# Attention with v as scaled float16 pairs, the logits kept in other tiles, and x's rows split at other steps

## The chip, the cores and the metric

The kernel runs on one core of a Trainium2 chip. The metric is the device time of one execution in microseconds (us); the median of the runs stands for the kernel. The trace is that of one further execution, taken by the hardware profiler. Engines: PE is TensorE (PEld its weight loads), DVE is VectorE, ACT is ScalarE, POOL is GpSimd; SPq is the queue in which SyncE issues the transfers (DMAs).

## What is computed

Attention with a decay, an MLP with h·cos(h), and a dense mixture of eight experts whose gates are made doubly stochastic:

```python
scores = scale * q @ k.T + (cum[:, None] - cum[None, :])   # causal; 4 batches, 8 heads, 576 rows, 64 columns
x = softmax(scores) @ v                                    # -> 2304 x 512
h = x @ w_in                                               # 512 -> 2048
x = (h * cos(h)) @ w_out                                   # 2048 -> 512
P = sinkhorn(exp(x @ w_gate))                              # 2304 x 8, eight rounds
out = sum(P[:, e:e+1] * (relu(x @ w1[e]) @ w2[e]) for e in range(8))
```

The answer is in float32, so the large matmuls split each operand into a high and a low half and add three products (hi·hi, hi·lo, lo·hi).

## The kernel before, in words

There are three stages. **Attention** handles 16 pairs of heads, seven steps to a pair, 112 steps in all. Steps 0 to 5 of a pair are the row tiles [0, 1], [2], [3] of head 0 and then of head 1; step 6 is the last 64 rows of both heads. The loop over x (from L818) writes out by hand what each engine does at a step: `on_pe`, `on_act`, `on_dve`, then `go("pool", x)`. Every engine works in its written order, and an instruction that waits holds up all that are behind it on its engine. The table `PREP` (L516) says at which step before or after its own first step (that of pair 0 in the second place) and on which engine each piece of a pair's preparation is emitted.

For pair n, `load_pair(n + 2)` (L341 on, with the copies at L330, L336 and L340) is emitted at the pair's step 2: ten DMAs in the SP queue, four for q, three for k, three for v. Ahead of it in the same step and the same queue stands `dq1` (L553), a DMA that copies what ACT wrote by `qhi1` (L489, the 640 columns of the second head of q, emitted one step earlier). The raw v lies in one of three tiles. `square_v` (L466) squares v on ACT and sums it into a column of `vsum`; it is emitted four steps ahead of its pair. `split_v` (L448) makes three bfloat16 parts of v on POOL in five instructions. `weigh` (L673) multiplies the two float16 halves of the attention weights with those parts, five matmuls to a block of 128 by 128 (L701); the last 64 rows go in float32 (L681). `norm` (L704) divides by the row sums.

```python
"v_sq": (("act", -4), ("act", -3)),
"ld": (("pool", 2), ("pool", 2)),
ACT_ORDER = ("XEH", "EXH", "EXH", "XHE", "XEH", "XEH", "XEH")
```

In these letters X is the preparation, E the exponentials of the next step (L639), H the high half of the weights of this step (L663, L659).

Between the steps, `pieces` prepares the MLP's weights: `read_unit` (L168) reads 64-bit words into float32 with four DVE instructions for each of two halves (L175, L177, L179, L182, with a product on POOL at L174), and after the third of them asks for the next weights by `load_job` (L122, L127), a DMA in the SP queue that waits until DVE has read the staging tile. One unit of weights takes some four pairs. `chunk_scale` and `split_row` (L223) scale and split x, the MLP's input, on POOL, as each of the five chunks of rows becomes complete; a chunk has four row blocks, three POOL instructions each.

**The MLP** runs 80 items (4 blocks of units, 5 chunks, 3 to 5 units) in order: `layer1` (12 matmuls, L263), `between` (ACT and DVE, L282 to L290), `layer2` two items later (12 matmuls, L943). The first two `layer1` are emitted in the last attention steps. `survey` (L893) reads the experts' weights for their largest values into the two tiles `seen`. In the last block `logits` (L991) multiplies x by the gate's weights and copies the result into a tile `lg`, which lies in `tmw1` or `tmw2`, tiles of the weight reader; `logits2` (L1005) turns it.

**The experts** start with POOL alone: `prepare_alone` (L1208 to L1271) splits the first four parts of the experts' weights, and `combine_first` (L1291 to L1295) makes seven sums of x blocks, all in POOL's written order. Their tiles lie in the memory that the MLP's tiles leave. The tile of the second part, `wa01`, lies on bytes 148256 to 155424 of a partition; on the same bytes lay the end of `xl1` (134240 to 150624, the operand of `logits` for chunks 1 and 3), `tmw1` (150624 to 154720) and the start of `tmw2` (from 154720).

Of the kernel before, what the change touches and what calls it, by code (L numbers as in the profile page):

```python
# [23 lines left out]
def kernel(  # L24
# [75 lines left out]
    wsum = [big.tile([P, 2], F32, name=f"wsum{i}") for i in range(3)]  # L100
    vsum = big.tile([P, B * HP], F32, name="vsum")
    xsum = big.tile([P, NCH], F32, name="xsum")
    bk_w, sc_w = [big.tile([P, NUM, 2], F32, name=nm) for nm in ("bkw", "scw")]
    bk_x, sc_x = [big.tile([P, NCH], F32, name=nm) for nm in ("bkx", "scx")]
    both, lift = [big.tile([P, NUM], F32, name=nm) for nm in ("both", "lift")]
# [187 lines left out]
    with tc.manual_schedule():  # L293

        with ExitStack() as actx:
# [20 lines left out]
            K1 = [ap1.tile([P, S], F32R, name=f"k1_{i}") for i in range(4)]  # L316
            K2 = [ap1.tile([P, S], F32R, name=f"k2_{i}") for i in range(4)]
            E4 = ap1.tile([P, SP], F32, name="e4")
            vraw = [ap1.tile([P, NQ, 2, D + 1], F32, name=f"vraw{i}") for i in range(3)]
            qraw = [ap1.tile([P, NQ, 2 * D], F32, name=f"qr{i}") for i in range(2)]  # L320
            kraw = [ap1.tile([P, NQ, 2 * D], F32, name=f"kr{i}") for i in range(2)]
# [110 lines left out]
            nc.gpsimd.memset(qraw[1][LAST:P, NQ - 1, 0:D], 0.0)  # L432
            for t in (kraw[1], xpt):
                nc.gpsimd.memset(t[LAST:P, NQ - 1, :], 0.0)
            for i in range(3):
                nc.gpsimd.memset(vraw[i][:, :, :, D : D + 1], 1.0)
                nc.gpsimd.memset(vraw[i][LAST:P, NQ - 1, :, :], 0.0)
# [7 lines left out]

            vs_of, tr_of = {}, {}

            def split_v(n):  # L448
                vr = raw[n][2]
                v1 = ap2.tile([P, NF, 2, D + 1], BF16, tag="v1", name="v1")  # L450
                v23 = ap2.tile([P, 2, NF, 2, D], BF16, tag="v23", name="v23")
                rest = ap1.tile([P, NF, 2, D], F32, tag="tmp", name="vrest")
                vs_of[n] = (v1, v23[:, 0], v23[:, 1])
                nc.gpsimd.tensor_scalar(v1, vr[:, 0:NF], 1.0, 0.0, ALU.mult, ALU.add)
                nc.gpsimd.tensor_tensor(rest, vr[:, 0:NF, :, 0:D], v1[:, :, :, 0:D], ALU.subtract)
                yield
                nc.gpsimd.tensor_scalar(v23[:, 0], rest, 1.0, 0.0, ALU.mult, ALU.add)
                nc.gpsimd.tensor_tensor(rest, rest, v23[:, 0], ALU.subtract)
                yield
                nc.gpsimd.tensor_scalar(v23[:, 1], rest, 1.0, 0.0, ALU.mult, ALU.add)  # L460
                done.add(("v", n))
                yield

# [29 lines left out]
            def lo_in(n, which, h):  # L493
# [32 lines left out]
                "dk0": (("pool", -5), ("dve", -4)),  # L526
                "ql0": (("dve", -7), ("dve", -4)),
                "kl0": (("pool", -5), ("dve", -4)),
                "sp0": (("pool", -3), ("pool", -3)),
                "sp1": (("pool", -2), ("pool", -2)),  # L530
                "ql1": (("dve", -5), ("dve", -2)),
                "sp2": (("pool", -2), ("pool", -2)),
                "v_sq": (("act", -4), ("act", -3)),
                "ld": (("pool", 2), ("pool", 2)),
                "x_act": (("act", 11), ("act", 11)),
                "dq0": (("dma", -7), ("pool", -4)),
# [136 lines left out]
            def weigh(x):  # L673
                n, y = divmod(x, PS)
                h, ts = KIND[y]
                A = A_of.pop(x)
                if h is None:
                    for hh in range(2):
                        for kt in range(NQ):
                            c = kt * P + hh * LAST  # L680
                            nc.tensor.matmul(  # L681
                                pv_of[n, 1][0:LAST, NF + hh, :], A[:, c : c + LAST], raw[n][2][:, kt, hh, :],
                                start=kt == 0, stop=kt == NQ - 1,
                            )
                    return
                if ts[0] == 0:
                    bank = ps_o.tile([P, 512], F32, tag="o", name="pv")
                    spare_bank[:] = [lambda: bank[:, (NF + 2) * (D + 1) :]]
                    pv_of[n, h] = bank[:, 0 : (NF + 2) * (D + 1)].rearrange("p (t d) -> p t d", d=D + 1)
                need(("v", n))  # L690
                v1, v2, v3 = vs_of[n]
                c = 0
                for t in ts:
                    todo = []
                    for kt in range(t + 1):
                        hi, lo = A[:, 0, c : c + P], A[:, 1, c : c + P]
                        w1, w2, w3 = v1[:, kt, h, :], v2[:, kt, h, :], v3[:, kt, h, :]
                        todo += [(hi, w1), (hi, w2), (hi, w3), (lo, w2), (lo, w1)]
                        c += P
                    for y, (a, w) in enumerate(todo):  # L700
                        nc.tensor.matmul(  # L701
                            pv_of[n, h][:, t, 0 : w.shape[1]], a, w, start=y == 0, stop=y == len(todo) - 1
                        )

            def norm(n, h):
                if h == 0:
                    xp_of[n] = xpt
                xp, pv = xp_of[n], pv_of.pop((n, h))
                rc = RC[h]
                parts = [(P, 0, NF, xp[:, 0:NF, h * D : (h + 1) * D], ESC)]  # L710
                if h == 1:
                    parts.append((LAST, NF, NF + 2, xp[0:LAST, NF, :].rearrange("p (h d) -> p h d", h=2), 1.0))
                for m, t0, t1, _, esc in parts:
                    nc.vector.tensor_scalar(rc[0:m, t0:t1, :], pv[0:m, t0:t1, D : D + 1], 1e-9 * esc, None, ALU.add)
                nc.vector.reciprocal(rc, rc)
                for m, t0, t1, dst, _ in parts:
                    nc.vector.tensor_tensor(
                        dst, pv[0:m, t0:t1, 0:D], rc[0:m, t0:t1, :].to_broadcast([m, t1 - t0, D]), ALU.mult
                    )
# [16 lines left out]
            def put(n, key, fn, *args):  # L736
                eng, step = PREP[key][n == 0]
                ON["pool" if eng == "dma" else eng].setdefault(n * PS + step, []).append((RANK[key], fn, args))
# [14 lines left out]
            for n in range(NPAIR):  # L753
                if n:
                    put(n, "aug", aug, n)
                put(n, "q_pe", turn_in, n, 0)
                put(n, "k_pe", turn_in, n, 1)
                for h in range(2):
                    put(n, f"qhi{h}", hi_in, n, 0, h)
                    put(n, f"khi{h}", hi_in, n, 1, h)  # L760
                    put(n, f"dq{h}", dup_in, n, 0, h)
                    put(n, f"dk{h}", dup_in, n, 1, h)
                    put(n, f"ql{h}", lo_in, n, 0, h)
                    put(n, f"kl{h}", lo_in, n, 1, h)
                if "pool" in (eng_of(n, "kl0"), eng_of(n, "kl1")):
                    put(n, "ktc", keep_k, n)
                put(n, "sp0", start_split, n)
                put(n, "sp1", more_split, n)
                put(n, "sp2", more_split, n)
                put(n, "v_sq", square_v, n)  # L770
                put(n, "ld", load_pair, n + 2)
                put(n, "x_pe", turn_x, n)
                put(n, "x_act", keep_x, n)
            pieces = chain(chain.from_iterable(run_unit(u) for u in range(NWA)), read_unit(NWA), scale_unit(NWA))
            scaling = iter(())
            rows = []
            for j, (_, b1) in enumerate(BATCHES):
                first_step = (HP * b1 + HP - 1) * PS
                for x in range(KD):
                    rows.append((max((HP * b1 + x) * PS + 12, first_step + 1), j, x))  # L780
            rows.sort()

            def on_pe(x):
                for z in PE_ORDER[x % PS]:
# [18 lines left out]
            def on_dve(x):  # L803
                n, y = divmod(x, PS)
                for z in DVE_ORDER[x % PS]:
# [8 lines left out]
                    if z == "O" and 0 <= x < NSTEP:  # L814
                        lo_a(x)

            ahead = {}
            for x in range(-9, NSTEP + PS):  # L818
                for n, when in enumerate((NSTEP - 2, NSTEP + 1)):
                    if x == when:  # L820
                        ahead[n] = layer1(*items[n])
                on_pe(x)
                if x == NSTEP + 2:
                    between(*items[0], ahead[0])
                on_act(x)
                on_dve(x)
                go("pool", x)
                quiet[0] = x % PS in (1, 2, 4, 5) or x >= NSTEP
                for j, (_, b1) in enumerate(BATCHES):
                    if x == (HP * b1 + HP - 1) * PS - 3:  # L830
                        scaling = chain(scaling, chunk_scale(j))
# [3 lines left out]
                    next(scaling, None)  # L835
                if rows and rows[0][0] <= x:
                    split_row(*rows.pop(0)[1:])
                if x == NSTEP - 2:
                    quiet[0] = True
                    for _ in scaling:  # L840
                        pass
                    for u in range(NWA):
                        turn_factors(u, 0, NCH)
                    block_factors(0)
                    down_factors(0, 0, NCH)
            quiet[0] = True
            for _ in pieces:
# [138 lines left out]
        def logits(j, xt, step, bank):  # L986
            n = CH[j][1]
            ps = bank()
            for kk in range(KD):
                for s in range(2):  # L990
                    nc.tensor.matmul(  # L991
                        ps[:, 0:n], wg_of[0][:, kk, :], xt[:, s, kk, :], start=kk + s == 0, stop=kk == KD - 1 and s == 1
                    )
            lg = tmw[j % 2 + 1][:, 0:512]
            nc.scalar.copy(lg[0:16, 0:n], ps[0:16, 0:n])
            if step is not None:
                at(after_l2, step, lambda: logits2(j, lg, bank))
# [77 lines left out]
            at(after_l2, 73 + x // 2, lambda x=x: scale_first(x))  # L1075
        pieces = work()
        for n in range(len(items) + LAG):
            if n < len(items):
                ps = ahead.pop(n) if n in ahead else layer1(*items[n])
            for fn in after_l1.pop(n, []):  # L1080
# [625 lines left out]
```

## Time and profile before

| | |
|---|---|
| median of 3 runs | 2045.49 us (2044.63 to 2045.53) |
| the profiled execution | 2045.4 us, its span in the trace 2043.7 us |
| PE, PEld busy | 95%, 68% of the span |
| DVE, ACT, POOL busy | 72%, 59%, 55% |
| attention | to about 252 us |
| MLP | to about 655 us |
| experts | to the end |

Busy time is counted over the whole span, and the three stages have different limits. A matmul's end is modelled, so a PE that is shown as busy need not be at its peak.

### The profile page before, as it was taken

To read this page: it belongs to the slowest core of one execution; us is meant where nothing else is said; L and a number is where in the kernel's file an instruction comes from. 1 tells how busy PE (TensorE), PEld (TensorE's weight loads), DVE (VectorE), ACT (ScalarE), POOL (GpSimd) and SP (SyncE) were. 2 spreads that over 40 slices of the span, in tenths; PEclk is the share of its full clock that TensorE was granted. 3 is DMA by queue.
4 is the path that set the end of the run, shared out by engine and by line. 5 is a ranking of instruction groups with operands and counts; after the bars stand their busy time and mean duration, and the time that the engine had idled before them with its cause. 6 is when DMAs were issued, how large, how long until landed. Compare 5 with 4: busy or idle time off the path is not lost.

```text
span 2043.7 us, 39956 instructions
## 1 busy us (share of the span) xinstructions
PE 1949.8 (95%) x15098; PEld 1393.0 (68%) x15098; DVE 1473.5 (72%) x3237; ACT 1212.3 (59%) x2449; POOL 1126.0 (55%) x1528
## 2 busy tenths in 40 slices
PE   7999989999997489999999999999999999999998
PEld 6888745454543266777777777777777777777776
DVE  8888767786565247878777777777777777777776
ACT  7888778777643266555555555555555555555543
POOL 7888854423022988546555555465555555655531
PEclk9999999999999689999999999999999999999999
DMA  5435255454300202120220211212202122022022
GB/s 130 109 89 116 53 175 176 155 165 125 114 11 11 85 33 100 41 86 32 76 75 22 86 46 62 86 32 76 76 22 86 33 75 86 22 83 78 12 86 63
DMA packets 133921, 157.59 MB, mean 77 GB/s; under 512 B 63840, under 2 KB 98016, under 8 KB 133728
## 3 DMA queue, kind: packets, MB, share of 16 engines
q1 hardware_dynamic: 133728, 155.03, 25.0%
q8 instruction: 119, 1.95, 0.4%
q14 instruction: 74, 0.61, 0.1%
HBM read 139.71 MB, written 10.37 MB: 73 GB/s over the span
## 4 chain that ended last, share of the span: by engine, by line
PE 77%; DVE 7%; POOL 7%; ACT 6%; issue 2%; DMA 0%; SPq 0%; DVEq 0%; POOLq 0%; ACTq 0%
PE y L1571 18%; PE y L1450 17%; PE bq L1571 14%; PE bq L1450 13%; PE ph L263 5%; PE a L943 5%; PE pv L701 1%; PE pst L651 1%; DVE ph L287 1%; ACT t L285 1%; DVE acc L959 1%; PE pss L594 1%; DVE t L284 1%; PE pss L595 1%; DVE tmw L182 1%
## 5 line engine op out<-in xcount | busy, mean ns | idle before, releaser
L1571 PEld LDWEIGHTS <-h 128*128 128x128 f16 x6048 | 592.7, 98 | 87.1 <-POOL h L1485 10.8
L1450 PEld LDWEIGHTS <-wa 128*128 128x128 f16 x4032 | 395.7, 98 | 294.9 <-issue 43.1
L1450 PE MATMUL y<-xc,wa 128*128 128x384 f16 x2304 | 434.5, 328 | 31.4 <-POOL xc L1291 26.6
L1485 POOL TENSOR_TENSOR h<-rt,h 128x384 f16<-128x384 f32 x192 | 175.7, 915 | 449.2 <-ACT h L1484 441.4
L1571 PE MATMUL y<-wb,h 128*128 128x256 f16 x3456 | 410.5, 273 | 10.0 <-POOL h L1485 10.0
L1466 ACT ACTIVATE ct<-y 128x384 f32<-128x384 f32 x192 | 94.4, 491 | 451.5 <-PE y L1450 451.5
L1450 PE MATMUL bq<-xc,wa 128*128 128x384 f16 x1728 | 331.3, 328 | 1.1 <-POOL xc L1292 1.0
L1571 PE MATMUL bq<-wb,h 128*128 128x256 f16 x2592 | 308.2, 273 | 0.2 <-DVE h L1476 0.2
L1552 DVE SCALAR_TENSOR_TENSOR acc<-y,gate,acc 128x256 f32<-128x256 f32 x504 | 212.6, 477 | 48.7 <-PE y L1571 48.6
L943 PE MATMUL a<-H,w 128*128 128x512 f16 (+1 forms) x960 | 203.0, 359 | 9.3 <-ACT H L288 4.3
L263 PE MATMUL ph<-xt,w 128*128 128x512 f16 (+1 forms) x960 | 199.8, 358 | 0.0
L1552 DVE SCALAR_TENSOR_TENSOR acc<-bq,gate,acc 128x256 f32<-128x256 f32 x378 | 159.7, 478 | 39.2 <-PE bq L1571 39.1
L943 PEld LDWEIGHTS <-w 128*128 128x128 f16 x960 | 93.4, 98 | 105.5 <-issue 14.8
L1476 DVE TENSOR_TENSOR h<-bq,h 128x384 f16<-128x384 f32 x288 | 158.1, 551 | 3.2 <-ACT h L1473 0.6
L1470 DVE SCALAR_TENSOR_TENSOR bq<-bq,ct 128x384 f32<-128x384 f32 x192 | 107.7, 561 | 68.2 <-PE bq L1450 67.4
L1470 DVE SCALAR_TENSOR_TENSOR bq<-y,ct 128x384 f32<-128x384 f32 x96 | 54.3, 566 | 140.6 <-PE y L1450 135.3
L263 PEld LDWEIGHTS <-w 128*128 128x128 f16 x960 | 93.6, 99 | 89.5
L1473 ACT CAST h<-bq 128x384 f16<-128x384 f32 x288 | 134.6, 483 | 14.2 <-DVE bq L1527 14.0
L1479 POOL TENSOR_TENSOR h<-st,h 128x384 f16<-128x384 f32 x96 | 88.0, 917 | 84.1 <-ACT h L1473 80.2
L1483 ACT ACTIVATE rt<-bq 128x384 f32<-128x384 f32 x192 | 93.7, 488 | 27.8 <-DVE bq L1470 25.1
L1231 POOL TENSOR_TENSOR tm<-sg 128x256 f32<-128x256 f32 x128 | 92.3, 732 | 15.0 <-POOL h L1479 12.3
L1484 ACT ACTIVATE h<-bq 128x384 f16<-128x384 f32 x192 | 94.3, 491 | 0.0
(260 smaller groups left out, 3214.7 us busy)
## 6 DMA issues: line engine op xcount, KB each, us to landing
xc<-xd SPq DMA_DIRECT2D x105, 384.0 KB
seen<-in_moe_w_dram SPq DMA_DIRECT2D x64, 512.0 KB
sg<-in_moe_w_dram SPq DMA_DIRECT2D x64, 512.0 KB
stg<-in_moe_w_in_dram SPq DMA_DIRECT2D x16, 512.0 KB
stg<-in_moe_w_out_dram SPq DMA_DIRECT2D x16, 512.0 KB
xd<-xc SPq DMA_DIRECT2D x14, 384.0 KB
q<-q SPq DMA_DIRECT2D x30, 160.0 KB
out_dram<-acc SPq DMA_DIRECT2D x18, 256.0 KB
```

The source lines that it names most:

```text
L263: nc.tensor.matmul(ps[:, 0:n], w[:, ws, kk * P : (kk + 1) * P], XT[j][:, xs, kk, :], start=first, stop=kk == KD - 1 and (ws, xs) == PASSES ...
L943: nc.tensor.matmul(a_of[b, j][x][:, 0:n], w[:, s1, DM + x * P : DM + (x + 1) * P], H[:, s2, 0:n], start=i == 0 and n_ == 0, stop=end and n ...
L1450: nc.tensor.matmul(ps[:, 0:HN], w[:, ws, a, k, :], X[b][:, xs, k, :], start=fresh and n == 0, stop=n == 5, skip_group_check=not fresh,)
L1466: nc.scalar.activation(c, cut(ps), AF.Copy, scale=RAISE)
L1470: nc.vector.scalar_tensor_tensor(cut(c), cut(ps), RAISE, other, ALU.mult, ALU.add)
L1473: nc.scalar.copy(HT[m][c][:, 0, :], src)
L1476: nc.vector.tensor_tensor(HT[m][c][:, 1, :], src, HT[m][c][:, 0, :], ALU.subtract)
L1483: nc.scalar.activation(r, cut(ps), AF.Relu)
L1484: nc.scalar.activation(HT[m][c][:, 0, :], cut(ps), AF.Relu)
L1485: nc.gpsimd.tensor_tensor(HT[m][c][:, 1, :], r, HT[m][c][:, 0, :], ALU.subtract)
L1552: nc.vector.scalar_tensor_tensor(a, v, gate[:, tt, e : e + 1], a, ALU.mult, ALU.add)
L1571: nc.tensor.matmul(ps[:, at_ * HD : (at_ + 1) * HD], HT[m][a][:, s1, c * P : (c + 1) * P], W2T[side][m][:, s2, b, :], start=fresh and m == ...
```

## The change

v is no longer split into three bfloat16 parts. A power of two per pair of heads (`scale_v`, from the pair's sum of squares: one matmul with a matrix of ones, one DVE and three POOL instructions) scales it, and two float16 parts are made in three POOL instructions. `weigh` then needs three matmuls to a block, and `norm` takes the scale into the row sums. The sum of squares is emitted eight steps ahead of the pair instead of four, the scale six steps ahead. `lg` lies in the `seen` tiles. The row blocks of x come one to a pair; those of the last chunk are split in the MLP, after the first layer of items 1, 3, 5 and 7. The factors for the MLP's first block are written at two earlier steps (98 and 109) in place of step 110. The two small new tiles in `big` move the tiles behind them by 128 bytes.

```diff
+    bk_v, sc_v = [big.tile([P, B * HP], F32, name=nm) for nm in ("bkv", "scv")]
...
+            v_hi = [ap1.tile([P, NF, 2, D + 1], F16, name=f"vh{i}") for i in range(2)]
+            v_lo = [ap1.tile([P, NF, 2, D], F16, name=f"vl{i}") for i in range(2)]
...
+            def scale_v(n):
+                assert n == 0 or quiet[0]
+                ps = total(vsum[:, n : n + 1], 10)
+                for _ in make_scale(ps, sc_v[:, n : n + 1], bk_v[:, n : n + 1]):
+                    pass
+
             def split_v(n):
                 vr = raw[n][2]
-                v1 = ap2.tile([P, NF, 2, D + 1], BF16, tag="v1", name="v1")
-                v23 = ap2.tile([P, 2, NF, 2, D], BF16, tag="v23", name="v23")
-                rest = ap1.tile([P, NF, 2, D], F32, tag="tmp", name="vrest")
-                vs_of[n] = (v1, v23[:, 0], v23[:, 1])
-                nc.gpsimd.tensor_scalar(v1, vr[:, 0:NF], 1.0, 0.0, ALU.mult, ALU.add)
-                nc.gpsimd.tensor_tensor(rest, vr[:, 0:NF, :, 0:D], v1[:, :, :, 0:D], ALU.subtract)
+                vh, vl = v_hi[n % 2], v_lo[n % 2]
+                whole = ap1.tile([P, NF, 2, D], F32, tag="tmp", name="vrest")
+                vs_of[n] = (vh, vl)
+                nc.gpsimd.tensor_scalar(whole, vr[:, 0:NF, :, 0:D], sc_v[:, n : n + 1], 0.0, ALU.mult, ALU.add)
                 yield
-                nc.gpsimd.tensor_scalar(v23[:, 0], rest, 1.0, 0.0, ALU.mult, ALU.add)
-                nc.gpsimd.tensor_tensor(rest, rest, v23[:, 0], ALU.subtract)
+                nc.gpsimd.tensor_scalar(vh[:, :, :, 0:D], whole, 1.0, 0.0, ALU.mult, ALU.add)
                 yield
-                nc.gpsimd.tensor_scalar(v23[:, 1], rest, 1.0, 0.0, ALU.mult, ALU.add)
+                nc.gpsimd.tensor_tensor(vl, whole, vh[:, :, :, 0:D], ALU.subtract)
...
-                "sp0": (("pool", -3), ("pool", -3)),
+                "sp0": (("pool", -3), ("pool", -2)),
...
-                "v_sq": (("act", -4), ("act", -3)),
+                "v_sq": (("act", -8), ("act", -3)),
+                "v_sum": (("pool", -6), ("pool", -3)),
...
-                        w1, w2, w3 = v1[:, kt, h, :], v2[:, kt, h, :], v3[:, kt, h, :]
-                        todo += [(hi, w1), (hi, w2), (hi, w3), (lo, w2), (lo, w1)]
+                        w1, w2 = v1[:, kt, h, :], v2[:, kt, h, :]
+                        todo += [(hi, w1), (hi, w2), (lo, w1)]
...
+                        nc.vector.tensor_scalar(rows_, den, 1e-9 * esc, sc_v[0:m, n : n + 1], ALU.add, ALU.mult)
...
+                put(n, "v_sum", scale_v, n)
...
-            for j, (_, b1) in enumerate(BATCHES):
-                first_step = (HP * b1 + HP - 1) * PS
-                for x in range(KD):
-                    rows.append((max((HP * b1 + x) * PS + 12, first_step + 1), j, x))
-            rows.sort()
+            rows = [((HP * b + HP + x) * PS - 1, b, x) for b in range(B - 1) for x in range(KD)]
+            assert BATCHES == [(0, 0), (0, 1), (1, 2), (2, 3), (3, 3)]
+            rows += [(NSTEP - PS + z, B - 1, x) for x, z in enumerate((4, 6, PS + 1, PS + 5))]
...
-                if x == NSTEP - 2:
-                    quiet[0] = True
-                    for _ in scaling:
-                        pass
+                if x == NSTEP - 2 * PS:
+                    block_factors(0)
                     for u in range(NWA):
-                        turn_factors(u, 0, NCH)
-                    block_factors(0)
+                        turn_factors(u, 0, 3)
+                if x == NSTEP - 3:
+                    assert not list(scaling)
+                    for u in range(NWA):
+                        turn_factors(u, 3, NCH)
                     down_factors(0, 0, NCH)
...
-            lg = tmw[j % 2 + 1][:, 0:512]
+            lg = seen[j % 2][:, 0:512]
...
         for n in range(len(items) + LAG):
+            if n in (1, 3, 5, 7):
+                split_row(NCH - 1, n // 2)
```

## Rows read from the trace of the kernel before

**Rows 1.** Busy time by stretch: engine busy (instructions), PE clock, DMA share, GB/s.

```profile
16.00:220.00 204.00, 187.82 (x2541) 170.44 (x2540) 176.27 (x511) 176.96 (x353) 170.73 (x203) 0.99 0.49 111
...
260.00:280.00 20.00, 16.67 (x89) 8.88 (x87) 12.89 (x22) 13.56 (x30) 12.31 (x13) 0.91 0.47 148
```

**Rows 2.** Timeline of PE: start, duration, instructions merged; one step's matmuls with v.

```profile
131.66 0.77 PE L701 MATMUL pv<-v,A 128*128 128x65 bf16 x20
```

**Rows 3.** Groups by line in 100 to 200 us: busy, mean ns, idle; POOL.

```profile
L458 POOL TENSOR_TENSOR vrest<-vrest,v 128x512 f32<-128x512 f32 x7 | 8.2, 1172 | 0.6
...
L141 POOL TENSOR_SCALAR bkx<-bkx 128x1 int32<-128x1 int32 x2 | 0.5, 234 | 0.2
```

**Rows 4.** Timeline of the SP queue: copies of q and loads, three pairs.

```profile
37.41 1.66 SPq L330 DMA_DIRECT2D qr<-in_q_dram  x2
...
135.36 0.50 SPq L553 DMA_DIRECT2D q<-q  x1
135.91 1.19 SPq L330 DMA_DIRECT2D qr<-in_q_dram  x2
...
142.55 0.63 SPq L340 DMA_DIRECT2D vraw<-in_v_dram  x1
...
212.31 1.32 SPq L330 DMA_DIRECT2D qr<-in_q_dram  x2
...
218.20 0.63 SPq L340 DMA_DIRECT2D vraw<-in_v_dram  x1
```

**Rows 5.** Two loads of v: issue and use in the timeline, and a later stretch's DMA.

```profile
8.54 0.61 SPq L340 DMA_DIRECT2D vraw<-in_v_dram  x1
...
11.28 0.74 ACT L466 ACTIVATE sq<-vraw 128x640 bf16<-128x640 f32 x1 [0.18 <-DMA vraw<-in_v_dram]
...
28.32 0.63 SPq L340 DMA_DIRECT2D vraw<-in_v_dram  x1
...
30.40:30.60 0.20, 0.20 (x5) 0.19 (x4) 0.20 (x1) 0.08 (x1) 0.20 (x2) 1.00 0.01 0
```

**Rows 6.** Timeline of ACT in four pairs.

```profile
103.00 0.79 ACT L639 ACTIVATE E<-E,nm 128x128 f32<-128x128 f32 x2
...
106.43 0.70 ACT L489 ACTIVATE q<-psq 64x640 fp32r<-64x640 f32 x1
...
118.27 0.62 ACT L184 ACTIVATE sq<-tmw 128x512 bf16<-128x512 f32 x1
...
138.66 0.72 ACT L466 ACTIVATE sq<-vraw 128x640 bf16<-128x640 f32 x1
...
139.50 0.49 ACT L663 ACTIVATE A<-pst 128x384 f16<-128x384 f32 x1
...
144.64 0.79 ACT L639 ACTIVATE E<-E,nm 128x128 f32<-128x128 f32 x2
```

**Rows 7.** Timeline of the SP queue behind those: a load of MLP weights, then q's.

```profile
152.30 0.40 SPq L122 DMA_DIRECT2D stg<-in_moe_w_in_dram  x1
...
153.34 1.25 SPq L330 DMA_DIRECT2D qr<-in_q_dram  x2
```

**Rows 8.** Timeline at the start of attention.

```profile
16.02 0.85 ACT L639 ACTIVATE E<-E,nm 128x128 f32<-128x128 f32 x2 [3.91 <-DVE nm L633]
...
16.16 0.63 SPq L340 DMA_DIRECT2D vraw<-in_v_dram  x1
```

**Rows 9.** Timeline between attention and MLP.

```profile
257.95 2.11 PE L943 MATMUL a<-H,w 128*128 128x384 f16 x12 [1.69 <-ACT acc L731]
...
265.47 1.09 DVE L182 SCALAR_TENSOR_TENSOR tmw<-dm,tmw 128x512 f32<-128x512 bf16 x1 [3.09 <-POOL dm L174]
...
268.97 3.65 PE L943 MATMUL a<-H,w 128*128 128x384 f16 x12 [2.63 <-ACT H L288]
```

**Rows 10.** Timeline between MLP and experts.

```profile
647.73 0.50 PE L991 MATMUL pl<-xl,wg 128*128 128x512 f32 x1 [0.17 <-DVE xl L977]
...
653.01 0.99 POOL L1258 TENSOR_SCALAR wa<-sg 128x512 f16<-128x512 f32 x2 [79.17 <-PE pl L1005]
```

More of the change, by code (lines that the diff above doesn't have):

```diff
@@ L434 @@
                 nc.gpsimd.memset(t[LAST:P, NQ - 1, :], 0.0)
+            for t in v_hi:
+                nc.gpsimd.memset(t[:, :, :, D : D + 1], 1.0)
             for i in range(3):
@@ L690, in weigh @@
                 need(("v", n))
-                v1, v2, v3 = vs_of[n]
+                v1, v2 = vs_of[n]
                 c = 0
@@ L713, in norm @@
                 for m, t0, t1, _, esc in parts:
-                    nc.vector.tensor_scalar(rc[0:m, t0:t1, :], pv[0:m, t0:t1, D : D + 1], 1e-9 * esc, None, ALU.add)
+                    rows_, den = rc[0:m, t0:t1, :], pv[0:m, t0:t1, D : D + 1]
+                    if esc == 1.0:
+                        nc.vector.tensor_scalar(rows_, den, 1e-9, None, ALU.add)
+                    else:
+                        nc.vector.tensor_scalar(rows_, den, 1e-9 * esc, sc_v[0:m, n : n + 1], ALU.add, ALU.mult)
                 nc.vector.reciprocal(rc, rc)
@@ L775 @@
             scaling = iter(())
-            rows = []
-            for j, (_, b1) in enumerate(BATCHES):
-                first_step = (HP * b1 + HP - 1) * PS
-                for x in range(KD):
-                    rows.append((max((HP * b1 + x) * PS + 12, first_step + 1), j, x))
-            rows.sort()
+            rows = [((HP * b + HP + x) * PS - 1, b, x) for b in range(B - 1) for x in range(KD)]
+            assert BATCHES == [(0, 0), (0, 1), (1, 2), (2, 3), (3, 3)]
+            rows += [(NSTEP - PS + z, B - 1, x) for x, z in enumerate((4, 6, PS + 1, PS + 5))]
             def on_pe(x):
@@ L815, in on_dve @@
                         lo_a(x)
+            spare_bank.append(lambda: ps_h.tile([P, 512], F32, tag="h", name="ps1"))
             ahead = {}
@@ L821 @@
                         ahead[n] = layer1(*items[n])
+                quiet[0] = x % PS in (1, 2, 4, 5) or x >= NSTEP
                 on_pe(x)
@@ L827 @@
                 go("pool", x)
-                quiet[0] = x % PS in (1, 2, 4, 5) or x >= NSTEP
                 for j, (_, b1) in enumerate(BATCHES):
```

## The prediction

> **What bounds the kernel now.** I read the table of stretches first, then the timelines of each engine and of the SP queue in attention, then the two seams between the stages. In attention no engine stands out: of 204 us PE is busy 188, ACT 177, DVE 176, POOL 171 [rows 1]. So less work on one of them is worth something only where that one ends a wait. MLP and experts are bound by PE outside their seams and the change leaves their matmuls alone; there only the seams count. One more resource has no busy column: the chain from SP's loads to their landing. It repeats once a pair, and the change ties ACT into it.
>
> **The change, part by part.**
>
> *Fewer matmuls with v.* Twenty take 0.77 us, the last one's own 0.19 of pipeline left out about 0.58, so 0.03 each [rows 2]. Sixteen pairs drop 2 of 5 matmuls for 20 blocks: 640, or 1.2 us a pair on PE. *POOL* loses one subtraction of 1.17 and one conversion a pair and gains three small instructions of 0.23 [rows 3]: about 1 us less. *Scale:* one small matmul and one DVE instruction a pair; DVE stands for a few tenths until PE has finished that step, and behind it wait the next row maxima. All of this costs and gives nothing as long as another chain sets the pair's length; if none did, the gain would end where ACT stands, since ACT loses no work.
>
> *The square of v, four steps earlier.* This is the part that I take to decide. v's three loads are the last of ten, and they are issued at the pair's step 2. Now ACT reads v at step 6, ahead of that step's exponentials, and everything of ACT waits behind it: exponentials, the high halves for PE and DVE, and qhi1. On qhi1 waits dq1 in the SP queue, and behind dq1 stand the next ten loads: in the trace dq1 at 135.36 and the first load at 135.91 [rows 4]. That closes a ring, one turn a pair:
> - loads: from the first to the end of the last issue 7.27 in one pair and 6.52 in the last one [rows 4]; I take 6.85;
> - landing: at the start ACT began 2.1 us after the end of the issue (9.15 to 11.28, waiting for that DMA); in a later pair the issue ended at 28.95 and the DMA engines stood at 0.01 busy by 30.40, so not under 1.45 [rows 5]. I take 1.75, the middle;
> - the square itself: 138.66 to 139.50, 0.84 [rows 6];
> - ACT from the exponentials to the end of qhi1: 103.00 to 107.13, 4.13 without a gap [rows 6], then 0.55 to the first load [rows 4].
>
> Sum 14.1. In two of every four pairs a piece of weight work of some 0.65 lies in that stretch of ACT (such as that at 118.27 [rows 6]). In a third one the SP queue has a load of MLP weights ahead of dq1 that waits for DVE: 144.64 to 153.34, 8.70 instead of 4.68 [rows 6, 7]. The wait for v can use up some of that; between 4.68 (all) and 8.70 (nothing) I take 8.0, since DVE's own chain to that load is not shortened. So four pairs take 4·14.1 + 2·0.65 + 3.3 = 61.0, or 15.25 a pair. Before, twelve pairs took 37.41 to 212.31, 14.58 each [rows 4]. There the ring had slack, because v was squared four steps later. Price: 12·0.68 = **+8.1**. Its ends: with 6.52, 1.45 and 4.68 a pair takes 13.8, or 9 us less in all; with 7.27, 2.1 and 8.70 it takes 16.2, or 20 more.
>
> The Trainium skill's page DMA: Bandwidth & Descriptors, section Anatomy of one DMA, says that a DMA has a fixed cost of about 2.0 us, most of it the receipt of the last write. The wait at the start (2.1) agrees with it. By its figure the ring would be 0.25 longer and the sum, as an estimate, some 3 us higher.
>
> *Start.* Pair 1's square now stands ahead of ACT's first exponentials, which began at 16.02; its v is issued to 16.79 [rows 8]. Landing 18.54, square to 19.4: **+3.4** (0 if PE's and DVE's first work covers it, 3.8 with a landing of 2.1). *End.* The last two pairs wait for no load and have PE's and POOL's lighter work: **-0.5** (-3 to +1).
>
> *The rows of x and the factors.* Before, eight row blocks stand on POOL at the end. DVE's weight reading waits 3.09 for POOL behind them and holds up the MLP's own steps; PE waits 1.69 and 2.63 [rows 9], and behind these waits its clock is granted at 0.91 over 20 us, which at the lower of its two levels (1.2 in place of 2.4 GHz) is 1.8 us lost [rows 1]. Together 6.1. Four blocks now go into the MLP between items 1 and 7, where POOL has gaps, and there each can hold up one product that DVE waits for; I leave 0.8 for that: **-5.3** (-6.1 to -2).
>
> *The logits' tile.* POOL stands 79 us until logits2 has read lg, and goes on at 653.01 [rows 10]; from there to the first expert work it is POOL that ends PE's waits. With lg elsewhere the same bytes still belong to the end of xl1, whose last reader is the logits matmul that ends at 648.23 [rows 10]; the 128 bytes do not change that overlap. So POOL starts 4.8 earlier, less a semaphore: **-4.7** (0 if another wait takes its place).
>
> *Sum* against the profiled execution's 2045.4 (span 2043.7 and 1.7 around it; the median is 0.1 above): 3.4 + 8.1 - 0.5 - 5.3 - 4.7 = +1.0, so 2046.4; the DVE waits for the scale inside the ring's long pair I put at 0.6 more: **2047.0**. A measurement of this kernel can tell about 0.2%, 4.1 us; this lies within.
>
> **Rivals.**
>
> *Landing as slow as at the start.* Place: ACT at step 6. Price: 2.1 in place of 1.75 is 0.35 in each of 12 pairs and once more at the start, 4.6, and a long pair that absorbs nothing adds 0.7 three times, 2.1. That gives 2053.7, slower. It decides from a ring of about 15.5 a pair on. For it: the one wait for v that the trace shows is 2.1. Against it: then the queue also held the start's other loads.
>
> *The ring has slack.* If SP issues in 6.5 and the data land in 1.5, a pair takes about 14.6 and attention keeps its time but for the start; the seams give their 10: 2038, faster. For it: rows 4 show 6.52 once. Against it: nothing in the change makes SP quicker.
>
> *PE and POOL bound attention.* Then 1.2 us a pair of PE's and 1 of POOL's go, and perhaps 0.7 a pair shows, 11 in all: with the seams 2024, faster. For it: PE's 188 of 204. Against it: the wait for the load, which would have to end before ACT gets to it.
>
> *The logits' tile does nothing*, since another reader of those bytes ends as late: 2051.7, slower. Against it: xl1 is the only other late one.
>
> **How the numbers follow.** The forecast has 0.44, of which 0.36 within the bound and 0.08 above it; slow landing 0.21; slack 0.16; PE and POOL 0.14; the tile 0.05. The slack and PE and POOL end faster, slow landing and the idle tile slower. That makes 0.30 faster, 0.36 the same, 0.34 slower. The range runs from 2035 to 2057: it takes in the slack's 2038 and the slow landing's 2053.7 with some 3 us for the start and the end, and leaves out the fourteen hundredths of PE and POOL and the far end of the ring. The forecast's own range is 2042 to 2051.
>
> **What would show it.** Right: ACT waits for DMA vraw at L466 by 0.5 to 2 us in most pairs, first loads of consecutive pairs 15 us apart, the first exponentials near 19.4; attention's last matmul some 11 later; no wait over 1 us for POOL's product at the first MLP items; POOL's wait before the second part of the weights ended by the logits matmul L991 (its new line) and not by logits2, about 650 us on the new clock. Wrong: no wait for v at L466 and pairs under 14.2 us; a POOL that waits for logits2 as before; or PE held up in the MLP by row blocks of the last chunk.

## The result, and the profile after

| | before | after |
|---|---|---|
| median of 4 runs each | 2045.51 us (2044.63 to 2045.61) | 2057.43 us (2055.70 to 2057.86) |
| ratio | | 1.0058, 95% interval 1.0040 to 1.0075 |
| the profiled execution, its span | 2045.4, 2043.7 | 2055.7, 2054.0 |
| attention's last matmul with v ends | 251.6 | 268.2 |
| layer 1 of the MLP's item 6 (first with 512 columns) | 276.70 | 292.99 |
| first matmul of the experts | 670.39 | 680.60 |

The change makes the kernel slower by 0.58%, 11.9 us; the sum had 1.6. The profiled executions differ by 10.3, and the table says where: 16.6 are lost by the end of attention, 0.3 come back at the seam to the MLP, 1.4 during the MLP (not followed further), 4.7 at the seam to the experts.

*Attention.* The groups of waits of the changed kernel over twelve pairs (engine, line, what it waited for: us in total, times, longest):

```profile
POOL bkv L142 <- DVE bkv L137: 37.5, 12, 8.3
DVE q L508 <- ACT q L497: 20.3, 12, 3.6
ACT sq L474 <- DMA vraw<-in_v_dram: 13.7, 8, 2.9
PEld pst L660 <- ACT E L648: 12.8, 15, 2.8
```

The third line is the predicted one: ACT waits for v, in eight of the twelve pairs, by 0.2 to 2.9 us. The second and the fourth are those who wait for ACT. The first was not in the sum: POOL stands for the new scale, once a pair. The chain of work that ended last (followed back from the last instruction, each time to what released it) passes over a load of v in eleven of the twelve pairs (2.24 to 3.41 us from the start of its issue), in the kernel before and in e1 (below) in none. In three of the four pairs without a wait v lands 0.5 to 0.7 us ahead of the square, while ACT still has other work; there the ring is all but closed. One turn of the ring, in the timelines of the SP queue and of ACT (start, duration; in brackets the idle time before):

```profile
103.51 1.26 SPq L333 DMA_DIRECT2D qr<-in_q_dram  x2
...
110.21 0.63 SPq L343 DMA_DIRECT2D vraw<-in_v_dram  x1
...
112.81 0.74 ACT L474 ACTIVATE sq<-vraw 128x640 bf16<-128x640 f32 x1 [2.86 <-DMA vraw<-in_v_dram]
...
113.54 0.78 ACT L648 ACTIVATE E<-E,nm 128x128 f32<-128x128 f32 x2
...
116.96 0.70 ACT L497 ACTIVATE q<-psq 64x640 fp32r<-64x640 f32 x1
...
118.24 1.20 SPq L333 DMA_DIRECT2D qr<-in_q_dram  x2
```

Loads 7.33 (103.51 to 110.84), landing 1.97 (to 112.81), square 0.73, ACT from the exponentials to the end of qhi1 4.12 (113.54 to 117.66), to the next first load 0.58: 14.73. These pieces fill the distance between the two first loads by their making; what matters is that from the square to the end of qhi1 the timeline shows no idle time of ACT. The 7.33 is no fixed price: two of v's issues took 1.97 in this turn and 0.93 to 1.09 in nine of the twelve, and all ten loads took 6.14 to 7.37. The lines that answer to [rows 4] and [rows 8]:

```profile
18.64 0.74 ACT L474 ACTIVATE sq<-vraw 128x640 bf16<-128x640 f32 x1 [6.78 <-DMA vraw<-in_v_dram]
...
19.38 0.78 ACT L648 ACTIVATE E<-E,nm 128x128 f32<-128x128 f32 x2
...
42.08 1.33 SPq L333 DMA_DIRECT2D qr<-in_q_dram  x2
...
226.31 1.26 SPq L333 DMA_DIRECT2D qr<-in_q_dram  x2
...
232.47 0.63 SPq L343 DMA_DIRECT2D vraw<-in_v_dram  x1
...
235.99 0.74 ACT L474 ACTIVATE sq<-vraw 128x640 bf16<-128x640 f32 x1 [3.24 <-DMA vraw<-in_v_dram]
```

The first exponentials stand at 19.38 (16.02 before), and twelve pairs take 184.2 us, 15.35 each (14.58 before). The last two lines show one more wait for v, 3.24 us, behind the last load.

*Attention to MLP*, the timelines of POOL, DVE and PE, against [rows 9], and a row of the table of stretches (columns of [rows 1]):

```profile
276.81 1.22 POOL L227 TENSOR_SCALAR acc<-acc,scx 128x512 f32<-128x512 f32 x1
...
285.28 1.04 POOL L175 TENSOR_TENSOR dm<-stg 128x512 bf16<-128x512 f32 x1
...
286.35 0.69 DVE L183 SCALAR_TENSOR_TENSOR tmw<-dm,tmw 128x512 f32<-128x512 bf16 x1 [3.71 <-POOL dm L175]
...
277.44 0.32 PE L956 MATMUL a<-H,w 128*128 128x384 f16 x1 [0.72 <-ACT H L289]
...
281.77 2.11 PE L956 MATMUL a<-H,w 128*128 128x384 f16 x12
...
289.24 3.77 PE L956 MATMUL a<-H,w 128*128 128x384 f16 x12 [3.41 <-ACT acc L970]
...
289.00:293.00 4.00, 3.76 (x15) 1.89 (x15) 2.38 (x4) 3.70 (x8) 3.83 (x5) 0.57 0.37 151
```

From 276.81 to 285.28 POOL has no gap: a row block of the last chunk, then the halves of a unit of weights; only then the product that DVE waits for. The stall has moved by some items and is as large as before: from the end of attention to item 6 it takes 24.8 us, before 25.1. The part that the prediction gave to the clock stays too: behind the wait of 3.41 us twelve matmuls take 3.77 us instead of the 2.11 of the same form at 281.77, and the granted clock of 289 to 293 us is 0.57 in the mean, near the lower of its two levels.

*MLP to experts*, against [rows 10]:

```profile
663.27 0.99 POOL L1273 TENSOR_SCALAR wa<-sg 128x512 f16<-128x512 f32 x2 [74.49 <-PE pl L1004]
```

POOL now goes on behind the logits matmul (662.67 to 663.17), no longer behind logits2, and PE's wait for the first combined block is 10.10 in place of 14.83.

### The profile page after: what moved, and what is told of

Read it like the earlier page. It is cut to its first block, busy times and chain, and to the rows that moved or that the text cites. A ratio compares the mean times of both kernels' runs of the same rounds, so it can differ in the third digit from the quotient of the medians.

```text
span 2054.0 us, 38769 instructions
## 1 busy us (share of the span) xinstructions
PE 1953.0 (95%) x14490; PEld 1386.2 (67%) x14490; DVE 1474.0 (72%) x3253; ACT 1212.3 (59%) x2449; POOL 1108.3 (54%) x1549
## 3 DMA queue, kind: packets, MB, share of 16 engines
q1 hardware_dynamic: 133728, 155.03, 24.8%
## 4 chain that ended last, share of the span: by engine, by line
PE 80%; DVE 7%; ACT 5%; POOL 3%; DMA 2%; issue 2%; SPq 0%; ACTq 0%; DVEq 0%; POOLq 0%
PE y L1586 18%; PE y L1465 17%; PE bq L1586 14%; PE bq L1465 13%; PE ph L264 6%; PE a L956 6%; DMA vraw<-in_v_dram 2%; PE pst L660 1%; ACT E L648 1%; DVE A L680 1%; PE pv L710 1%; PE pss L603 1%; ACT t L286 1%; DVE ph L288 1%; POOL xc L1307 1%
## 5 line engine op out<-in xcount | busy, mean ns | idle before, releaser
L1488 ACT CAST h<-bq 128x384 f16<-128x384 f32 x288 | 134.6, 483 | 14.2 <-DVE bq L1542 14.1
L1498 ACT ACTIVATE rt<-bq 128x384 f32<-128x384 f32 x192 | 93.7, 488 | 27.5 <-DVE bq L1485 24.8
```

The lines of the kernel that those rows point to most:

```text
L1488: nc.scalar.copy(HT[m][c][:, 0, :], src)
L1498: nc.scalar.activation(r, cut(ps), AF.Relu)
```

## The experiments

All in one table; the steps are those of v's square and of the scale against the pair's first step, "pair" the mean of twelve distances between first loads of q, as above. It is read from the one profiled execution, which can lie some us from the median (e10: 2048.4 against 2053.0). The kernel before ran again beside each group of experiments, with medians from 2044.8 to 2045.2 and single runs from 2041 to 2048. A ratio is that to the kernel before, with its 95% interval.

| run | square, scale at | v's loads | else | median us | ratio (interval) | pair |
|---|---|---|---|---|---|---|
| before | -4, none | last | | 2045.5 | 1 | 14.58 |
| after | -8, -6 | last | | 2057.4 | 1.0058 (1.0040 to 1.0075) | 15.35 |
| e10 | -8, -5 | last | | 2053.0 | 1.0040 (1.0025 to 1.0054) | 15.24 |
| e6 | -7, -6 | last | | 2042.7 | 0.9992 (0.9982 to 1.0001) | 14.75 |
| e11 | -7, -5 | last | | 2037.1 | 0.9961 (0.9946 to 0.9976) | 14.17 |
| e9 | -6, -6 | last | | 2035.6 | 0.9957 (0.9942 to 0.9972) | 14.21 |
| e1 | -6, -5 | last | | 2027.2 | 0.9913 (0.9896 to 0.9929) | 13.57 |
| e5 | -8, -6 | first | | 2036.7 | 0.9959 (0.9944 to 0.9974) | 14.38 |
| e12 | -8, -5 | first | | 2030.2 | 0.9931 (0.9916 to 0.9946) | 13.67 |
| e14 | -7, -5 | first | | 2031.5 | 0.9936 (0.9919 to 0.9952) | 13.87 |
| e2 | -8, none | last | before's all else | 2061.2 | 1.0075 (1.0058 to 1.0093) | 15.52 |
| e8 | -6, -5 | last | rows, tile as before | 2037.5 | 0.9965 (0.9951 to 0.9978) | 14.06 |
| e3 | -4, none | last | before, new tile | 2041.8 | 0.9981 (0.9971 to 0.9990) | 14.65 |
| e4 | -4, none | last | before, new rows | 2038.9 | 0.9973 (0.9961 to 0.9985) | 14.09 |
| e13 | -4, none | last | before, rows of three chunks | 2043.2 | 0.9992 (0.9983 to 1.0001) | 14.07 |
| e7 | -6, -5 | last | last chunk later | 2024.3 | 0.9893 (0.9875 to 0.9911) | 13.65 |
| e15 | -5, -5 | last | last chunk later | 2022.5 | 0.9891 (0.9876 to 0.9906) | 13.40 |

### Is it the ring?

**The square later, alone in before, and one step later** (here and below only the new lines are shown where no old line stands beside them).

```diff
# e1
+                "v_sq": (("act", -6), ("act", -3)),
+                "v_sum": (("pool", -5), ("pool", -3)),
# e2, in the kernel before
+                "v_sq": (("act", -8), ("act", -3)),
# e6
+                "v_sq": (("act", -7), ("act", -3)),
```

> The changed kernel with v's square at step -6 (behind the previous pair's copy of q) and the scale at -5, in place of -8 and -6. Theory (the ring of loads, landing, square, exponentials, copy of q): ACT no longer waits for v, the first exponentials come back to about 16, twelve pairs take at most 14.6 us each in place of 15.35; 9.3 in the pairs and 3.4 to 4.7 at the start come back, so about 2042 (2038 to 2044). Rival 1 (the scale's chain over PE, DVE and POOL lengthens the pairs, not v's landing): the chain is still there, so 2052 to 2056. Rival 2 (with the ring gone PE's and POOL's lighter work shows): pairs under 14.0 us, 2036 or less.

> The kernel before, with nothing changed but v's square at step -8 in place of -4. Theory (the ring): first exponentials at 19.4, pairs of 15.3 us, attention's last matmul 12 to 15 later, so 2057 to 2060 without any scale or float16. Rival 1 (the scale's chain): there is no scale here, so 2046 to 2048. Rival 3 (part of the loss is in the lighter PE and POOL work being in other places): between, 2050 to 2055.

> The changed kernel with v's square one step later, at -7, still ahead of the copy of the second half of q; the scale stays at -6. Theory (the ring, with its length as worked out): ACT's part shrinks by 1.6 us to about 2.5, so the ring has 12.6 us against a pair of 13.6 that PE and POOL ask for; it binds only behind a load of weights that is late, some 1 us in every fourth pair: 2031 (2027 to 2034). Rival 1 (any square ahead of that copy costs the whole): 2045 to 2057.

Two steps later the changed kernel is 30 us faster: 2027.2, 18 less than before. The theory had 2042; what came was its rival 2 on top of it (pairs of 13.57, 2036 or less). Over twelve pairs no engine waits for v any more, POOL waits for k, and PE, ACT and POOL are busy for 152, 153 and 134 of 163 us. The timelines of ACT and the SP queue in e1, and its table of stretches with the columns of [rows 1]:

```profile
16.25 0.85 ACT L648 ACTIVATE E<-E,nm 128x128 f32<-128x128 f32 x2 [4.41 <-DVE nm L642]
...
38.10 1.24 SPq L333 DMA_DIRECT2D qr<-in_q_dram  x2
...
200.93 1.23 SPq L333 DMA_DIRECT2D qr<-in_q_dram  x2
```

```profile
38.10:200.93 162.83, 151.71 (x1767) 134.55 (x1764) 146.23 (x454) 153.28 (x307) 133.93 (x188) 1.00 0.49 112
```

The square moved alone in the kernel before, without any scale or float16, costs some 16: the theory's 2057 to 2060 with 1.2 over, the first exponentials at 19.24, attention's end 17.7 later where 12 to 15 were expected. So the early square alone loses more than the whole change does. The step to -7 missed both of its forecasts (2031; 2045 to 2057): it gave only half of what it should have by the ring's length, which left some 12 us open; in its trace ACT waits for v for 2.7 us in all over twelve pairs, but POOL for the scale for 30.5.

**The ring cut at another place**, v's loads ahead of q's and k's:

```diff
                 if n < NPAIR:
-                    load_qk(n)
                     load_v(n)
+                    load_qk(n)
```

> The changed kernel as it is (square at step -8), but with v's three loads ahead of those of q and k in each pair. Theory (the ring): v's landing leaves the ring by the 4.7 us that q's and k's issues take, so ACT waits for v no longer and pairs come to about 13.6 us as with the late square; 2026 to 2031. Rival 1 (a square that stands ahead of the copy of q on ACT costs in itself, wherever v's loads are): 2045 to 2057. Rival 2 (q and k, 1.9 us later, become the new wait): 2035 to 2045.

20.7 us of the 30 come back with the square left at -8: so most of the loss is v's landing, and not the square as such. The time lies in the range of rival 2 and not in the theory's; the missing 9.5 were open between two causes, the scale's place and the later loads of q and k.

### The scale's place

```diff
# e9                                                # e11: -7 and -5; e12: v first, -8 and -5
+                "v_sq": (("act", -6), ("act", -3)),
# e10
+                "v_sum": (("pool", -5), ("pool", -3)),
# e14: v first, -7 and -5
```

> The changed kernel with the late square (-6) but the scale where the change has it (-6). Theory 1 (v's landing is all that held the pairs, by the ring): as with both late, 2027 (2025 to 2029). Theory 2 (the scale at -6 is a second hold: POOL's small instructions wait there for DVE's end of the step and stand ahead of the copy of k): 2038 to 2043, as in the run with the square at -7, and POOL waits some 3 us a pair for DVE L137.

> The changed kernel with the square where the change has it (-8) and the scale one step later (-5). Theory 1 (the ring alone): ACT still waits for v, pairs 15.2 to 15.4 us, 2052 to 2057. Theory 2 (the scale's place is the larger hold): 2030 to 2045. Theory 3 (both, the longer one hides the other): 2050 to 2056, no gain or 1 to 5 us, with the landing wait of ACT as before.

> The changed kernel with the square at -7 and the scale at -5. Theory 2 or 3 (the 15 us that the run with -7 and -6 lacked against -6 and -5 are the scale's place): 2027 to 2031. If they were the square's (a square ahead of the copy of q): 2040 to 2043.

> The changed kernel with v's loads ahead of q's and k's, the square at -8, the scale at -5. Theory 2 or 3: the 9.5 us that v first lacked against the late square are the scale's place, so 2027 to 2030. If q's and k's later loads were what it lacked: 2035 to 2038.

> The changed kernel with v's loads first, the square at -7 and the scale at -5. Of the 9.9 us that -7 lacked against -6 (v's loads last), theory A (v's landing behind the late loads of every fourth pair, waits of up to 1.7 and what follows them) has all gone: 2027 to 2029. Theory B (ACT's order: a square ahead of the exponentials of step 0 holds them up, wherever v's loads are): 2033 to 2037.

At -6 the scale's POOL instructions come ahead of the copy of k in POOL's order and wait until DVE is through its step, at -5 behind that copy. The waits over twelve pairs of e9:

```profile
POOL bkv L142 <- DVE bkv L137: 23.6, 9, 4.8
PE pv L710 <- DVE xp L730: 6.8, 12, 1.4
```

In e1 this group is gone and "POOL k L560 <- ACT k L499: 10.8, 6, 4.4" leads. The edit moves the scale's matmul and its DVE instruction too; that it is POOL's order that costs is read from these waits and was not tried by itself. One step is worth 8.4 us with the square at -6, 5.6 at -7, 6.5 with v first (the intervals of that pair just touch), and 4.5 with the square at -8, where the intervals overlap: while the ring holds, it hides about half of it, if not all.

In e10 ACT still waits for v, in 11 of 12 pairs, 15.9 us in all. Its 2053.0 fits theories 1 and 3 alike; against theory 1 stand the 8.4 us between e9 and e1. So theory 3 is the one that is left, two holds one behind the other, the ring the longer. Two ranges were missed: e9's 2035.6 lies between those of its theories, e11's 2037.1 too. And e10 and e2 are not followed to the end: with pairs of 15.2 and 15.5 their chain of work passes over v's landing in only four and six of twelve pairs.

With both holds out of the way the runs with v first end at 2030.2 and 2031.5, and no difference shows there between the square at -8 and at -7; the interval of each overlaps that of the other. Of the 9.9 us between e11 and e1 some 5.6 go with v first, within the overlap of the intervals; e14 fell between what its two theories gave, and the rest up to e1 is some 4 us. For a part of these its trace has a wait that e1 has not, "PE psq L483 <- DMA qr<-in_q_dram: 2.0, 2, 1.1": with v first, q lands later (rival 2 of e5, at a small size). What remains was not settled.

### The other parts, each alone

```diff
# e3, in the kernel before
+            lg = seen[j % 2][:, 0:512]
# e4, in the kernel before: the change's rows and factors, and
+            if n in (1, 3, 5, 7):
+                split_row(NCH - 1, n // 2)
# e13, in the kernel before
+                    old = max((HP * b1 + x) * PS + 12, first_step + 1)
+                    rows.append((old if j > 2 else (HP * j + HP + x) * PS - 1, j, x))
# e8: the changed kernel as e1, with rows, factors and lg of the kernel before
```

> The kernel before, with nothing changed but the logits' copy in the tiles of the survey. Theory: POOL starts on the second weights' part behind the logits matmul, 4.7 us earlier, and the experts with it: 2040.8 (2040 to 2042). Rival (another wait takes its place): 2045 to 2046.

> The kernel before, with nothing changed but the places of x's row blocks and of the first block's factors. As predicted (the stalls at the seam go): 2040.2. Theory after the result (the row blocks of the last chunk, in the MLP's items, hold up POOL's product once more and DVE with it; a wait of 3 to 4 us there in place of 2.63 and 1.69): 2044 to 2046.

> The kernel before with only the row blocks of the first three chunks one to a pair, at its step 6; the last two chunks' blocks and the factors as before. Theory (the 6 us of the run with all rows moved come from attention: a block at step 5 of the pair stands ahead of POOL's work that the weights' load and q's copy wait for, and it does so in every fourth pair): first loads as there, 2039 to 2041. Rival (they come from the last steps and the seam, as the prediction had it): 2043.5 to 2045.5.

> The kernel before with v as scaled float16 pairs and the late square, but x's row blocks, the factors and the logits' tile as before. If the parts add up (late square in all -18, rows alone -6.2, tile alone -3.3), the pairs give -8 to -9: 2036.5. If PE's and POOL's lighter work costs and gives nothing as the prediction's sum has it: 2045.5. If it gives all of PE's 1.2 us a pair: 2026.

*The tile* gives 3.9 us by its ratio (2.0 to 5.9); in the trace PE's wait at the experts falls from 14.83 to 10.13, the 4.7 of the sum. *The pairs* alone give 7.2. *The rows* alone give 5.5, but not where the prediction had it: attention ends at 245.9 (251.6 before) and the seam to item 6 takes 24.2 in place of 25.1. The theory after the result (2044 to 2046) was wrong as well, since it knew of the seam alone. e13 shows the two halves apart. Its 2043.2 lies between its two forecasts, and its interval reaches beyond 1, so the whole is not told apart from the kernel before; what follows is read from its trace. Its attention ends at 244.6. Waits of the kernel before over twelve pairs:

```profile
PE pv L701 <- POOL v L460: 6.1, 6, 1.7
PEld pss L595 <- POOL k L505: 3.9, 3, 1.3
ACT ktf L578 <- POOL v L460: 3.8, 3, 1.3
PE pss L595 <- POOL k L505: 3.3, 3, 1.1
```

In e13 the two groups of pss are gone, and the other two are 4.2 and 1.9. The cause stands in POOL's timeline of the kernel before, a row block (L226 to L164) right ahead of a copy of k; it is the second of three in one pair (the others at 120.07 and 136.16). Behind it POOL has no gap until the k that PE waits for (the last line, of PE):

```profile
125.99 0.58 POOL L226 TENSOR_SCALAR acc<-acc,scx 128x384 f32<-128x384 f32 x1
126.65 0.52 POOL L163 TENSOR_SCALAR xt<-acc 128x384 f16<-128x384 f32 x1
127.25 0.92 POOL L164 TENSOR_TENSOR xt<-acc,xt 128x384 f16<-128x384 f32 x1
128.26 0.67 POOL L551 TENSOR_SCALAR k<-k 64x576 fp32r<-64x576 f32 x1
...
142.49 0.39 PE L595 MATMUL pss<-k,q 128*128 128x256 f32 x1 [1.10 <-POOL k L505]
```

In e13 no block stands there, and three distances between first loads, one in every fourth pair, are 2.0 to 2.6 shorter (the others change by -1.0 to +0.8). A block right behind the last part of v, in front of the same work, stands in both kernels, at 136.16 and at 131.48, though it is emitted at step 5 of the pair before and at step 6 in e13. So what the trace shows is that the pair has one block and not three; the step within the pair, which e13's theory named, it does not show. More than half of the gain is lost again at e13's seam, since eight row blocks still stand there and attention has caught up with them: POOL comes to the factors (turnv) only behind six of them (ACT and PE, against [rows 9]):

```profile
250.56 0.67 ACT L282 ACTIVATE t<-ph,quarter,turnv 128x384 int32<-128x384 f32 x1 [7.60 <-POOL turnv L155]
...
254.92 4.00 PE L944 MATMUL a<-H,w 128*128 128x384 f16 x12 [5.75 <-ACT acc L731]
```

The seam takes 29.1 there. So the spread over the pairs gives the rows' gain, and what e4 has beyond e13 keeps it: the fourth chunk's blocks at other of the last steps, the last chunk's in the MLP, the factors earlier. Which of these three does it was not tried. By ratio pairs, rows and tile add up to 0.81%, and e1, which has them all, gains 0.87%.

### A version that beats both

```diff
# e7: e1, and
-            if n in (1, 3, 5, 7):
-                split_row(NCH - 1, n // 2)
+            if n in (5, 7, 8, 10):
+                split_row(NCH - 1, (5, 7, 8, 10).index(n))
# e15: e7 with
+                "v_sq": (("act", -5), ("act", -3)),
```

> Late square (-6, scale at -5), and the last chunk's row blocks behind the first layer of items 5, 7, 8 and 10 in place of 1, 3, 5 and 7. Theory (these blocks hold up POOL's product that DVE waits for): the waits of 2.75 and 1.0 + 0.5 us of PE at the first MLP items go, 3 to 4 us: 2023.5 (2022 to 2025). Rival (the halves of the weights, also POOL's, hold it up): 2026.5 to 2027.5.

> The version with the row blocks at items 5, 7, 8 and 10, and the square at -5, in the same step as the scale. If ACT has more room at step 2 than at step 1: 2021 to 2024. If the scale then waits for the square: 2025 to 2030. If neither: 2024.

In e1 PE's waits at the first items are 1.01, 0.51 and 2.75, in e7 0.65, 0.27 and 0.81:

```profile
254.68 0.69 DVE L183 SCALAR_TENSOR_TENSOR tmw<-dm,tmw 128x512 f32<-128x512 bf16 x1 [0.65 <-POOL dm L175]
...
257.57 2.11 PE L956 MATMUL a<-H,w 128*128 128x384 f16 x12 [0.81 <-ACT acc L970]
```

From the end of attention to item 6 it takes 20.5 us, against 23.0 in e1 and 25.1 before. The medians differ by 2.9, the intervals overlap; the trace is what shows it. e15 is 1.8 lower still, not told apart from e7, so its forecasts "2021 to 2024" and "2024" are not told apart either. Both are some 1.1% faster than before: 2022.5 is 23 us under it and 35 under the change as made.

## Why the prediction was wrong

The forecast's mechanism was right and the sign of its sum too, but the sum said 2047.0 and the time is 2057.4, just beyond the range's 2057. By its terms, against the profiled executions (the changed kernel's, 2055.7, is the fastest of its four runs; the median lies another 1.7 above it):

| term | predicted | measured |
|---|---|---|
| start (up to the first load at 42.08) | +3.4 | +4.7 |
| ring, twelve pairs, with DVE's waits for the scale | +8.1 and 0.6 | +9.3 |
| end of attention | -0.5 | +2.6 |
| seam to the MLP | -5.3 | -0.3 |
| seam to the experts | -4.7 | -4.7 |
| the MLP itself | 0 | -1.4 |

- *The step that failed most* is "Four blocks now go into the MLP between items 1 and 7, where POOL has gaps ... I leave 0.8 for that: -5.3". POOL has no gaps there: it also makes the halves of a unit of weights, and with a block ahead of them DVE waits 3.71 for its product and PE 3.41, with the clock's loss behind it. The prediction's own sign of being wrong, "PE held up in the MLP by row blocks of the last chunk", is what came. With the blocks at items 5 to 10, and the ring cut, the seam gives 4.6 (20.5 against 25.1); only the change of their items, from e1 to e7, is worth 2.5 of it.
- *"The last two pairs wait for no load"* failed too. Twelve distances between first loads hold twelve turns; the last load's own landing came behind them, 3.24 us. From the last first load to the end of attention it takes 41.9 us (39.3 before), 42.5 in e2 without a scale, and 37.3 in e1 with the late square.
- *The start* was right for the first exponentials (19.38 against 19.4); the pair behind it lost 1.3 more, since its v, too, was waited for (1.75).
- *The ring* was right as a mechanism: 15.35 a pair against 15.25, dq1 and the next loads behind a wait for v. That the means agree so well is in part luck: the three turns with a late load took 16.4 to 17.4, where the sum had 17.4, and the others 14.1 to 15.4, where it had 14.1 to 14.75. In the turn shown above the loads took 7.33 and the landing 1.97. Of the waits for v, four of eight were over the 2 us named. Of the nine waits over 1 us, the start's and the end's included, six give a landing of 1.72 to 2.04 us from the end of the last issue, three of 2.9 to 3.1. The Trainium skill's page DMA: Bandwidth & Descriptors, section Anatomy of one DMA, gives a fixed cost of about 2.0 us, for the path of the transfers that GpSimd issues; these loads are issued by SP. The six agree with that figure all the same, and it was nearer than the 1.75 taken. The rival of a slow landing thus had part of the truth.
- *"All of this costs and gives nothing as long as another chain sets the pair's length"* held, and its condition is what the runs show best: with the ring cut, the pairs give 7.2 us, and a pair that carries all parts takes 13.57. PE's and POOL's lighter work, a rival at 2024, is what e1 comes near at 2027, but by another split: the rival had 11 from the pairs and 10 from the seams, and the parts alone give 7.2, 5.5 from the rows (in attention) and 3.9 from the tile.
- *The scale* was put at 0.6 for DVE. By the waits it is POOL that pays: one step of the scale is worth 5.6 to 8.4 us with the square later or v first, and 4.5, not clear of the noise, with the ring as it is.
- *The rows in attention* were priced at nothing. PE's three waits for POOL's k, 3.3 us in all, stood in the waits of the kernel before, and one block to a pair in place of up to three was worth 6 to 7 us of attention with what follows them; the table of busy shares, from which I read that no engine stands out, does not show them.

## What to carry to other kernels

Where a step that reads a load is moved forward, add up the chain from that load's issue through the reader to whatever issues the next load: if it closes, its length is a floor for the period, however much other work is taken out. Then measure the parts apart, since a floor hides gains (here 18 us) as well as costs (the scale's place). And before small work is put on an engine "with gaps", list what that engine does in those very microseconds, with what waits behind it.

## Not expected of the hardware

The time from the end of the last issue to ACT's start on v was not one number: 1.72 to 2.04 us in six waits, 2.9 to 3.1 in three (232.47 and 235.99 above are one of them), in transfers of the same form. What lengthens the three was not tried.
